# Attention products of a recurrent layer as 64x64 tiles in one TensorE visit per group, states added up outside of the matmuls, outputs split from PSUM, and a new list schedule

## The chip, the core and the metric

The kernel runs on one core of one Trainium2 chip. The metric is the device time of one launch in microseconds (us), the median of several runs; less is better. A core has a matrix engine (PE, with its own weight loads, PEld), a vector engine (DVE), an activation engine (ACT), a general engine (POOL) and a queue engine (SP) that issues DMA transfers. SBUF is the on-chip memory of 128 partitions, PSUM the eight banks into which PE writes.

## What is computed

A recurrent attention over 4 batches, 8 heads, 768 tokens and 48 channels a head, whose outputs feed a feed-forward layer with a 3-tap convolution over the tokens and a gate:

```
for t in range(S):
    kt, vt, rt = (k[:, :, t], v[:, :, t], r[:, :, t])
    cur = np.einsum('bhd,bhe->bhde', u[None] * kt, vt)
    y[:, :, t] = np.einsum('bhd,bhde->bhe', rt, state + cur)
    state = w[None, :, :, None] * state + np.einsum('bhd,bhe->bhde', kt, vt)
...
h = np.maximum(x @ w_in, 0.0)          # x: y with heads side by side, (4, 768, 384); w_in 384x1024
hp = np.concatenate([zeros, h, zeros], axis=1)
for k in range(K):
    conv_out += conv_w[k][None, None, :] * hp[:, k:k + S, :]
gate = 1.0 / (1.0 + np.exp(-conv_out))
return h * gate @ w_out                # w_out 1024x384
```

All tensors are fp32 (the weights of the feed-forward layer come as fp64 and are converted on the chip). For the feed-forward products each operand is split into a high and a low part of 32 bits, and three products (high x high, high x low, low x high) are added up.

## The kernel before

**The work.** There are 24 attention groups: each is 128 tokens of one batch with all 8 heads, as two chunks of 64 tokens. Heads lie in four pairs p; one head of a pair lies on partitions 64 and up, the other from 0. The feed-forward layer runs over *units* of tokens: batch 0 in three units of about 256, batches 1 to 3 in two units of 384. A unit has 8 steps f, one for each 128 of the 1024 columns. Such a step is called an iteration here; there are 72, the first 24 of them on the narrow units.

**An iteration.** `first(i)` (line 666) issues 9 matmuls into a PSUM bank HP (two banks, in turn; line 682), then on ACT the relu (L686) and the middle tap (L687), on DVE the two outer taps (L690, two instructions), on ACT the sigmoid (L693), on DVE the gate product (L694, the last reader of HP), on ACT the high part GH (L696), and on DVE or POOL the low part GL. `second(i)` issues 9 matmuls into the three output banks PO (L711), three iterations behind. After the eighth step of a unit ACT copies PO to OS and SP stores it.

**A group of attention.** `load(g)` brings k and r with channels on partitions (KR), with tokens on partitions (KT), and v (WW). `prep(g)` multiplies KR by powers of the decay (DVE), copies r into the stacked operands RA and RB (a DMA from SBUF to SBUF), scales KT into KTA and KTB (two more of these DMAs from group 8 on), and puts the diagonal term into RA and RB by a select on POOL (L560). `scores(g)` is 16 matmuls of 48 rows on four quarters of PE (L578 to L581), into the banks psC and psS. `masked(g)` copies the scores into RA and RB under a mask, in four DVE instructions (L590). `state(g, c)` is 8 matmuls into psS (L602, L603), of 112 and 128 rows, in which the decay of the old state stands as extra rows; ACT then copies the new state into the operands WW (L609, two instructions), for each of the two chunks. `outputs(g, c)` is 8 matmuls of 112 and 128 rows (L618, L619) into psY. `yout(g)` copies psY to YY on ACT (L628), and for every second group six small DMAs inside SBUF bring the rows of the fourth head pair to their places, then ACT (L639) and DVE or POOL split the result into the two parts of XT, the input of `first`.

The matmuls of attention are plain fp32: each appears in the trace as two records of PE.

**Two banks are shared.** psS takes the second half of the scores and the state; the masked copies of that half also take the lock of the state's copy:

```
lock = ["psAu" if o else "psBu"] if ps is psS else []
op("dve", 0.34, [key, "mask"], [("Rs", i, nm, q)] + lock, lambda e, T=T, r=r, o=o, ps=ps, n=n, q=q: V.copy_predicated(
```

**What sets the order.** The kernel's program is written down by a planner (class `Plan`): each operation is recorded with a duration for each engine that may run it, what it reads and writes, and a matmul column count. `late()` gives every operation a due time back from a row of PE work, less an offset for its kind (table `OFF`); `order()` takes the operations one at a time, on the engine that can begin first. What stands on an engine is then in fixed order, and waits there for its own inputs. All DMAs are issued from SP. Operations marked `any` go to DVE or POOL. Until the first product of `second`, the planner fills gaps of PE with products of zeros (L768).

The first matmuls of `first` need the weights of step 0 converted (`convert`, lines 471 to 492: ACT L481, DVE L483 and L485, ACT L491, DVE or POOL) and the XT of the first two groups. The conversions of the 16 weight pieces run beside the first unit.

## Time and profile before

| | us |
|---|---|
| three runs | 336.68, 338.31, 340.29 |
| median | 338.31 |
| span of the profiled execution | 336.5 |
| busy in it: PE, DVE, ACT, POOL | 305.0, 261.1, 215.3, 181.6 |
| first matmul of `first` starts at | 43.5 |
| last matmul of `second` ends at | 332.9 |

The profile is of one execution, and its own time is given as the span, from its first instruction to its last; that lies 1.8 us under the median and 0.2 us under the fastest of the three runs. The span's parts are read by stretches of time, engine by engine; PEclk is the share of full speed at which PE was clocked. L682 and the like are lines of the kernel before. A duration in the profile includes the engine's start-up and end, which overlap with those of its neighbours, so sums of durations come out some per cent over the busy time.

### The profile page before, as it was taken

The page shows a single profiled execution, that of the slowest core. Times are in us where ns is not written, and L with a number is a line of the kernel's source. Part 1 is how long each engine was busy: PE and PEld are TensorE (multiplying, and loading weights), DVE is VectorE, ACT ScalarE, POOL GpSimd, SP SyncE. Part 2 cuts the span into 40 slices and gives each one's busy share as a digit, 9 for nine tenths or more (in the row PEclk, how much of TensorE's full clock was granted, in tenths as well). Part 3 has the DMA queues.
Part 4 walks back from the last instruction along what each step waited for, and adds up shares of the span by engine and source line. Part 5 has one row for each costly group of instructions (what it writes and reads, how often), then busy time and mean ns, then how long its engine had stood idle before and what let it go on. Part 6 is the DMA issues. An engine that isn't in the chain of part 4 may idle for free.

```text
span 336.5 us, 9895 instructions
## 1 busy us (share of the span) xinstructions
PE 305.0 (91%) x3894; PEld 284.2 (84%) x3894; DVE 261.1 (78%) x459; ACT 215.3 (64%) x515; POOL 181.6 (54%) x211
## 2 busy tenths in 40 slices
PE   7879688779989899999899979999999999999995
PEld 3667677778888788899899979988899999999995
DVE  6969779889989999988899876867776755655550
ACT  3565476766766675576667836586776666865751
POOL 7869766768789787768561444233220123433230
PEclk9789699779999999999999999999999999999999
DMA  6989687643484859677555640362311100200101
GB/s 172 264 219 266 163 234 202 212 126 101 132 224 124 239 130 238 193 195 220 137 150 135 196 120 0 104 196 71 106 49 36 50 0 10 75 1 2 71 0 70
DMA packets 25118, 44.02 MB, mean 131 GB/s; under 512 B 5296, under 2 KB 16176, under 8 KB 25072
## 3 DMA queue, kind: packets, MB, share of 16 engines
q1 hardware_dynamic: 25072, 43.40, 46.0%
q8 instruction: 30, 0.49, 0.7%
q14 instruction: 16, 0.13, 0.1%
HBM read 30.01 MB, written 4.72 MB: 103 GB/s over the span
## 4 chain that ended last, share of the span: by engine, by line
PE 51%; DVE 17%; DMA 14%; ACT 9%; issue 5%; SPq 2%; POOL 2%; ACTq 0%; DVEq 0%; POOLq 0%
PE HP L682 21%; PE PO L711 19%; DMA KR<-in_krd_dram 7%; DVE KR L351 3%; DVE CV L690 3%; PE psS L602 3%; ACT WW L609 3%; DMA WW<-in_vt_dram 3%; PE psY L618 3%; DVE TT L485 2%; DMA ST<-in_w_in_dram 2%; SPq L354 2%; DVE RB L590 2%; ACT SG L693 1%; DVE RA L590 1%
## 5 line engine op out<-in xcount | busy, mean ns | idle before, releaser
L682 PE MATMUL HP<-XT,wi 128*128 128x386 f32 (+3 forms) x648 | 116.2, 326 | 8.6 <-DVE SG L694 8.5
L682 PEld LDWEIGHTS HP<-XT,wi 128*128 128x128 f32 x648 | 103.7, 190 | 11.9 <-DVE SG L694 11.0
L711 PE MATMUL PO<-GH,wo 128*128 128x384 f32 (+3 forms) x432 | 110.9, 323 | 0.0
L690 DVE SCALAR_TENSOR_TENSOR CV<-HP,cw,CV 128x384 f32<-128x384 f32 (+3 forms) x144 | 80.5, 568 | 23.6 <-ACT CV L687 22.1
L351 POOL TENSOR_TENSOR GL<-SG,GH 128x384 fp32r<-128x384 f32 (+3 forms) x51 | 47.7, 936 | 86.6 <-ACT GH L696 76.2
L711 PEld LDWEIGHTS PO<-GH,wo 128*128 128x128 f32 x432 | 77.3, 192 | 0.2
L711 PE MATMUL PO<-GL,wo 128*128 128x384 f32 (+3 forms) x216 | 69.8, 323 | 1.0 <-POOL GL L351 1.0
L693 ACT ACTIVATE SG<-CV 128x384 f32<-128x384 f32 (+3 forms) x72 | 35.1, 489 | 38.5 <-DVE CV L690 38.0
L694 DVE TENSOR_TENSOR SG<-HP,SG 128x384 f32<-128x384 f32 (+3 forms) x72 | 36.5, 509 | 18.4 <-ACT SG L693 17.3
L686 ACT ACTIVATE HP<-HP 128x386 f32<-128x386 f32 (+3 forms) x72 | 31.8, 442 | 24.7 <-PE HP L682 23.7
L711 PEld LDWEIGHTS PO<-GL,wo 128*128 128x128 f32 x216 | 41.4, 192 | 1.4 <-POOL GL L351 1.4
L696 ACT CAST GH<-SG 128x384 fp32r<-128x384 f32 (+3 forms) x72 | 34.0, 475 | 13.3 <-DVE SG L694 13.3
L687 ACT ACTIVATE CV<-HP,cw 128x384 f32<-128x384 f32 (+3 forms) x72 | 39.2, 545 | 1.7
L351 DVE TENSOR_TENSOR KR<-KR,TKR 112x1024 f32<-112x1024 f32 (+1 forms) x26 | 33.9, 1313 | 5.4 <-DMA KR<-in_krd_dram 5.0
L609 ACT COPY WW<-psS 48x192 f32<-48x192 f32 x88 | 27.5, 313 | 7.6 <-PE psS L603 6.1
L618 PE MATMUL psY<-RA,WW 112*48 112x64 f32 x384 | 27.3, 228 | 0.0
L560 POOL TENSOR_SCALAR_AFFINE_SELECT RA<-QQ 64x512 f32<-64x512 f32 x24 | 17.8, 743 | 17.6 <-PE psY L619 11.9
L619 PE MATMUL psY<-RB,WW 128*48 128x64 f32 x384 | 27.3, 228 | 0.0
L602 PE MATMUL psS<-WW,KTA 112*48 112x48 f32 x352 | 25.6, 218 | 0.5 <-ACT QQ L541 0.5
L603 PE MATMUL psS<-WW,KTB 128*48 128x48 f32 x352 | 25.6, 218 | 0.0
L618 PEld LDWEIGHTS psY<-RA,WW 112*48 112x48 f32 x384 | 24.5, 130 | 0.8 <-issue 0.5
L602 PEld LDWEIGHTS psS<-WW,KTA 112*48 112x48 f32 x352 | 20.1, 129 | 5.9 <-issue 2.5
(93 smaller groups left out, 549.5 us busy)
## 6 DMA issues: line engine op xcount, KB each, us to landing
KR<-in_krd_dram SPq DMA_DIRECT2D x24, 448.0 KB, 4.8
KT<-in_krt_dram SPq DMA_DIRECT2D x16, 384.0 KB, 5.0
WW<-in_vt_dram SPq DMA_DIRECT2D x48, 96.0 KB, 2.8
out_dram<-OS SPq DMA_DIRECT2D x18, 192.0 KB, 1.9
ST<-in_w_in_dram SPq DMA_DIRECT2D x8, 384.0 KB, 4.8
ST<-in_w_out_dram SPq DMA_DIRECT2D x8, 384.0 KB, 4.4
RA<-KR SPq DMA_DIRECT2D x22, 96.0 KB, 4.2
RB<-KR SPq DMA_DIRECT2D x22, 96.0 KB, 4.3
```

The source lines that it names most:

```text
L351: op(eng, d, rd, wr, lambda e: e.tensor_tensor(**kw), cls, port=True)
L602: PE.matmul(psS[64:112, n:n + D], KTA[i][:, p, c, :], WA[i][:, p, c, :], start=True, stop=True)
L609: lambda e, T=T, ps=ps, o=o: A.copy(T[j][o:o + 48, :, cn, :], ps[o:o + 48, 0:NP * D].rearrange("q (p d) -> q p d", p=NP)), "WS")
L618: PE.matmul(psY[64:112, n:n + C], WA[i][:, p, c, :], RA[i][0:112, p, t], start=True, stop=True)
L682: PE.matmul(hp, wi[a][:, j, fs], X[:, x, j, t], start=(j == 0 and k == 0), stop=(j == 2 and k == 2))
L686: op("act", act(n) - 0.042, [], [H_], lambda e: A.activation(hp, hp, AF.Relu, scale=1.0 / WS))
L687: op("act", act(n) + 0.05, [H_, "cw"], [("T", ti)], lambda e: A.activation(t1, hp[:, 1:n + 1], AF.Copy, scale=cw[:, 3 * f + 1:3 * f + 2]), ...
L690: op("dve", dve(n + 60), [H_, "cw"], [("T", ti)], lambda e, k=k: V.scalar_tensor_tensor(out=t1, in0=hp[:, k:n + k], scalar=cw[:, 3 * f + k ...
L693: op("act", act(n), [("T", ti)], [("SG", ti)], lambda e: A.activation(sg, t1, AF.Sigmoid))
L694: op("dve", dve(n), [H_], [("SG", ti)], lambda e: V.tensor_tensor(out=sg, in0=hp[:, 1:n + 1], in1=sg, op=ALU.mult), "GG")
L696: op("act", act(n), [("SG", ti)], [("GH", gi)], lambda e: A.copy(gh, sg))
L711: PE.matmul(PO[m][:, :n], wo[a][:, f, ms], g2[x], start=(f == 0 and k == 0), stop=(f == NF - 1 and k == 2))
```

## The change

Nearly all of the attention part is written anew; the iterations of the feed-forward layer keep their instructions (their shapes go from 384/384 to 382/386 columns on the wide units). The outputs, the scores and the *additions* k'v of a chunk are all made of operands that start at partition 0 or 64 and fill at most a 64x64 quarter of PE. The state is no longer in a matmul: DVE adds the additions from PSUM to the faded old state (SD, made on ACT, POOL or DVE).

```
-            op("pe", SCD, [("KK", i), ("RR", i)], ["psAs", "psBs", "psAu", "psBu", "psA4", "psB4"], mm, "sc", 768, visit=vis(g - 1, ORDER[3]))
-            for ps, n, nm, o, key, q in ((psC, 0, "a", 0, "psAs", 0), (psC, 0, "b", 64, "psBs", 0),
-                                         (psS, 4 * C, "a", 64, "psA4", 2), (psS, 4 * C, "b", 0, "psB4", 2)):
...
-                        PE.matmul(psS[64:112, n:n + D], KTA[i][:, p, c, :], WA[i][:, p, c, :], start=True, stop=True)
-                        PE.matmul(psS[0:48, n:n + D], KTB[i][:, p, c, :], WB[i][:, p, c, :], start=True, stop=True)
...
-                    op("act", 0.21, [], ["psAu" if nm == "a" else "psBu", ("WS", j, cn, nm)],
...
-            op("act", 0.48, ["psY"], [("YY", n, k), ("YY3", n)], lambda e: A.copy(
-                y[0:112, :, k, :], psY[0:112].rearrange("q (p t) -> q p t", p=NP)))
...
+        def scores(n):
+                        mms.append((ps[o:o + 64, m:m + C], KR[i][o:o + 48, 0, p, t], KR[i][o:o + 48, 1, p, t], True, True))
+        def additions(n):
+                        mms.append((ps[o:o + 48, m:m + D], KV[i][o:o + 64, 0, p, c, :], KV[i][o:o + 64, 2, p, c, :], True, True))
+        def outputs(g):
+                        mms.append((ps[64 - o:112 - o, m:m + C], KV[i][o:o + 64, 2, p, c, :], RS[j][o:o + 64, 2 * p + c, :], True, not inter))
+                            mms.append((ps[64 - o:112 - o, m:m + C], SS[j][o:o + 48, c, p, :], KR[i][o:o + 48, 1, p, t], False, True))
+        def visit(cls, *parts):
+                for k in range(0, max(len(direct), len(cross)), 2):
+                    for y, a, b_, s0, s1 in direct[k:k + 2] + cross[k:k + 2]:
+                        PE.matmul(y, a, b_, start=s0, stop=s1)
+        def faded(dst, src, rd, key):
+                    for p in range(NP):
+                        A.activation(dst[:, p], src[:, p], AF.Copy, scale=PW[:, p, 64:65])
+            op("any", {"dve": dve(192), "pool": pool(192), "act": 0.54}, rd + ["PW2"], [key], mul, "SD", port=True)
+        def chain(g):
+            op("dve", 0.73, [ka, "mask"], [("RS", j)], lambda e: V.copy_predicated(
+                faded(SD[0], SS[j][:, 0], [("S", j, 0)], ("SD", 0))
+                op("dve", dps(192), [ku, ("SD", 0)], [("S", j, 1)], lambda e: V.tensor_tensor(
+                    out=SS[j][:, 1], in0=ps[:, 0], in1=SD[0], op=ALU.add), "S1")
...
+        def split(g):
+            op("act", act(512), [key], [("X", b % 2, gi)], lambda e: A.copy(X[0:112, 0, :, t], y), "XH")
+            op("dve", dps(512), [key, ("X", b % 2, gi)], [("XL", b % 2, gi)], lambda e: V.tensor_tensor(
+                out=X[0:112, 1, :, t], in0=y, in1=X[0:112, 0, :, t], op=ALU.subtract), "XL")
+            for k in range(3):
+                for o in (0, 64):
+                    dma(ks, [("XM", b % 2, h, k, o)], F[o + 48:o + 64, :, k, tu], F[o + 16 * k:o + 16 * k + 16, :, 3, tu],
+                        32, (gi + 1 - cuts[h]) * 512, 0.6, "XM", g < EARLY)
...
+            visit("V", (0, scores(g + 1)), (0, additions(g + 1)), (1, outputs(g)))
```

Scores and additions are *direct* (rows and columns from the same o, 0 or 64), outputs are *cross* (rows from o, columns from 64 - o); the last group of a batch has no second chunk of additions. So a full visit issues 64 matmuls, two direct and two cross ones in turn: the scores (bank psA) and additions (psU) of the next group beside the outputs (psY) of this one. There are no operands RA, RB, KTA, KTB and YY and none of their DMAs. The diagonal term is made by a select on POOL, by one product on DVE, or by eight small activations on ACT (`DG`); fading takes four small activations where it falls to ACT. The diagonal sum is made by the matmul way (`q`, 16 matmuls of one column) only for groups 2 to 5 (before: groups 0 to 7); the other groups make it on POOL and DVE. The six DMAs that move the fourth pair's rows come once a unit, on both parts of XT. Weights may be loaded from ACT's DMA queue too. Units are cut at whole groups less two tokens. The planner's durations, offsets (now by three phases) and tie rules are other numbers, and three first groups use the still free banks HP and PO.

Counted from the two programs: the wide and narrow iterations are the same, 648 matmuls into HP and 648 into PO. Attention has 384 score, 352 state, 384 output and 128 one-column matmuls before; after it has 1472 in the visits and 64 one-column ones.

On PE, at the middle of a visit of the steady part, there stood before (psY the outputs, psC and psS the scores):

```order
L618 MATMUL psY<-RA_62,WW_77 48x64
L619 MATMUL psY<-RB_65,WW_77 48x64
L578 MATMUL psC<-KR_69 64x64
L579 MATMUL psC<-KR_69 64x64
L580 MATMUL psS<-KR_69 64x64
L581 MATMUL psS<-KR_69 64x64
```

and now stands (KV the tokens' k, r and v; RS the masked scores; SS the state; x2 is the pair on rows 0 and 64):

```order
L530 MATMUL psY<-RS_67,KV_66 48x64 x2
L530 MATMUL psA<-KR_61 64x64 x2
L530 MATMUL psY<-KR_63,SS_71 48x64 x2
L530 MATMUL psU<-KV_64 48x48 x2
L530 MATMUL psY<-RS_67,KV_66 48x64 x2
```

The outputs moved between the scores and additions of the next group, in fours; the state's matmuls are gone.

On DVE, over about one group of the steady part, there stood before (RA and RB take the masked copies, CV the taps, SG the gate products):

```order
L690 SCALAR_TENSOR_TENSOR CV_91<-HP_122,cw,CV_91 128x384
L590 COPY_PREDICATED RA_62<-mask,psC 64x256
L590 COPY_PREDICATED RA_62<-mask,psS 64x256
L590 COPY_PREDICATED RB_65<-mask,psS 64x256
L694 TENSOR_TENSOR SG_94<-HP_122,SG_94 128x384
L590 COPY_PREDICATED RB_65<-mask,psC 64x256
L351 TENSOR_TENSOR XT_90<-YY_88,XT_90 128x3x128
L351 TENSOR_TENSOR GL_106<-SG_94,GH_101 128x384
```

and now stands:

```order
L294 TENSOR_TENSOR KR_63<-KR_63,TKR 112x512 x2
L616 TENSOR_TENSOR SG_80<-HP_109,SG_80 128x382
L555 TENSOR_TENSOR SS_72<-psU,SD_73 112x192
L547 COPY_PREDICATED RS_68<-mask,psA 128x512
L569 TENSOR_TENSOR XT_75<-psY,XT_75 112x4x128
L294 TENSOR_TENSOR GL_90<-SG_80,GH_85 128x382
L612 SCALAR_TENSOR_TENSOR CV_78<-HP_108,cw,CV_78 128x382
L559 TENSOR_TENSOR SS_71<-psU,SD_74 112x192
```

Four masked copies became one; two state additions and a split that reads psY came in.

At the beginning of DVE's program, behind the reciprocal of the decay's powers, there stood before:

```order
L440 RECIPROCAL TKR<-PW 112x4x32
L446 TENSOR_TENSOR uw<-uc,wc 48x4 x2
L351 TENSOR_TENSOR KR_67<-KR_67,TKR 112x512 x2
L426 TENSOR_TENSOR PW<-PW 112x4x32
L426 TENSOR_TENSOR PW<-PW 112x4x31
```

and now stands:

```order
L392 RECIPROCAL TKR<-PW 112x4x32
L294 TENSOR_TENSOR KV_64<-KV_64,uu 128x384
L294 TENSOR_TENSOR KR_61<-KR_61,TKR 112x512
L462 TENSOR_REDUCE QQ_69<-KV_64 128x8
L294 TENSOR_TENSOR KR_61<-KR_61,TKR 112x512
```

The first scaling of KR moved behind a product that reads POOL's product of the loaded k and r.

More of the change, by code (lines that the diff above doesn't have):

```diff
@@ L105, in op @@
         self.port.append(port)
-        if visit is not None:
-            self.visits.setdefault(visit[0], []).append(n)
-            self.visit[n], self.rank[n] = visit
+        self.phases.append(self.phase)
+        if port == 2 and self.phase == 0:
+            self.pins[n] = len(self.pins) - 1e3
         return n
@@ L149, in order @@
         tick, cols, warm = 0, 0.0, False
-        seq, where, when = [], [None] * n, [None] * n
-        fill, hist = FILL, []
-        lanes = [0.0] * 7
-        mode, cur, slack = 0, None, SLACK
-        todo_v = {v: set(m) for v, m in self.visits.items()}
-        ext = {}
-        for v, m in self.visits.items():
-            inner = set(m)
-            for i in range(n):
-                if any(j in inner for j in ops[i][2]) and any(i in ops[k][2] for k in m):
-                    inner.add(i)
-            ext[v] = {j for k in m for j in ops[k][2]} - inner
-        end_of = [None] * n
-        todo = n
+        seq, where, when, end_of = [], [None] * n, [None] * n, [None] * n
+        fill, hist, lanes, dq = FILL, [], {v: [0.0] * (self.LANES - 1) for v in ("sp", "act")}, 0.0
+        dqa = 0.0
+        shared = 0.0
+        mode, todo = 0, n
         while todo:
@@ new lines, in rwkv_ffn_kernel @@
+        op("dve", 0.07, [], ["wc1"], lambda e: V.memset(wc, 1.0))
+        for o in (0, 64):
+            dma(["wc1"], [("wc", o)], wc[o:o + 48], wd[64 - o:112 - o], 48, 16)
+        for i in range(NBUF):
+            op("pool", 1.0, [], [("KZ", i)], lambda e, i=i: e.memset(KR[i][32:64], 0.0))
+        load(0)
+        load(1)
+        op("dve", 0.274, [], ["wz"], lambda e: V.memset(wz, 0.0))
+        op("act", 1.5, ["wz"], ["sgt"], lambda e: A.activation(cw[:, 0:1], wz[:, 0:1], AF.Sigmoid))
+        def warm(e):
+            for k in range(NW):
+                PE.matmul((psY, psU, HP[1], PO[0], PO[2])[min(k, 4)], wz[:, :128], wz, start=True, stop=True)
@@ L751, in rwkv_ffn_kernel, with follow, visits @@
-        for i in range(NI + LAG):
-            if i < NI:
+                    dma([("OS", q)], [("out", u, m)], out[ms, b * S + t0:b * S + t0 + n], o, 128, 4 * n, cls="out")
+        made = [0]
+        def follow(g):
+            group_phase(g)
+            if g + 1 < NG and g + 1 >= APART:
+                chain(g + 1)
+            split(g)
+            if g + NBUF < NG:
+                load(g + NBUF)
+            if g + 2 < NG:
+                prep(g + 2)
+        def visits(n):
+            while made[0] < min(n, NG):
+                g = made[0]
+                made[0] += 1
+                group_phase(g)
+                if g + 1 < APART:
+                    visit("VA", (0, scores(g + 1)))
+                    visit("VU", (0, additions(g + 1)))
+                    visit("VY", (1, outputs(g)))
+                    chain(g + 1)
+                elif g + 1 < NG:
+                    visit("V", (0, scores(g + 1)), (0, additions(g + 1)), (1, outputs(g)))
+                else:
+                    visit("V", (1, outputs(g)))
+                follow(g)
@@ new lines, in rwkv_ffn_kernel @@
+        plan.phase = 0
+        w_in_piece(0)
+        conv_piece()
+        w_out_piece(0)
+        for o in (0, 64):
+            dma([], [("uc", o)], uc[o:o + 48], ut[o].rearrange("p d -> d p"), 24, 4)
+            op("dve", 0.07, [("wc", o), ("uc", o)], [("uw", o)], lambda e, o=o: V.tensor_tensor(
+                out=uw[o:o + 48], in0=uc[o:o + 48], in1=wc[o:o + 48], op=ALU.mult))
+        load(2)
+        plan.phase = 0
+        prep(0)
+        plan.phase = 0
+        visit("VA", (0, scores(0)))
@@ L753, in rwkv_ffn_kernel @@
+        visit("VU", (0, additions(0)))
+        chain(0)
+        prep(1)
+        for k in range(1, WPRE):
+            w_in_piece(k)
+        for i in range(NU * NF + LAG):
+            x = (i + LEAD) / NF
+            u = int(x)
+            dn = NEED[min(u + 1, NU - 1)] - NEED[min(u, NU - 1)]
+            visits(NEED[min(u, NU - 1)] + sum(x % 1 >= (k + 0.5) / dn for k in range(dn)))
+            if i < NU * NF:
                 first(i)
+            plan.phase = min(2, 1 + i // 3)
             if i + WPRE < NF:
```

604 lines of the change are left out of this document (243 added, 361 removed), and 6 rows, old and new, of the table OFF.

## The prediction

> **What bounds the kernel now.** I read the stretches of time first, cut at the first gate product's end (51 us), the end of the narrow iterations (148), the 45th of the 72 gate products (231) and the last product into HP (323). Columns: stretch and length, then busy us and count for PE, PEld, DVE, ACT and POOL, then the granted clock, the DMA share and GB/s.
>
> ```profile
> core 0: us, PE busy (x) PEld busy (x) DVE busy (x) ACT busy (x) POOL busy (x), PEclk, DMA share, GB/s
> 0.00:51.00 51.00, 39.23 (x697) 31.15 (x698) 40.35 (x69) 28.40 (x74) 38.98 (x53) 0.87 0.82 220
> 51.00:148.00 97.00, 85.91 (x1372) 80.04 (x1373) 88.84 (x163) 64.16 (x172) 76.56 (x88) 0.96 0.62 172
> 148.00:231.00 83.00, 78.22 (x926) 73.70 (x927) 69.88 (x122) 54.71 (x124) 38.16 (x42) 1.00 0.50 141
> 231.00:323.00 92.00, 91.74 (x855) 89.72 (x850) 58.92 (x102) 63.60 (x138) 26.42 (x28) 1.00 0.14 42
> 323.00:336.50 13.50, 9.93 (x57) 9.60 (x55) 3.16 (x6) 4.40 (x9) 1.52 (x2) 0.99 0.12 44
> ```
>
> The overall shares (PE 305.0 of 336.5) would name PE as the bound; the stretches say something else. From 51 to 148 DVE is the fullest (88.84 of 97 us) and PE idles for 11. From 231 on PE is full (91.74 of 92). In between both are loaded. So the span is DVE's time up to the 45th gate product, and after it the PE work that is left. Here is the joint: the gate product frees its HP bank, and the next but one product of `first` begins behind it.
>
> ```profile
> 50.41 0.42 DVE L694 TENSOR_TENSOR SG<-HP,SG 128x254 f32<-128x254 f32 x1 [1.23 <-ACT SG L693]
> ...
> 230.34 0.56 DVE L694 TENSOR_TENSOR SG<-HP,SG 128x384 f32<-128x384 f32 x1 [0.59 <-ACT SG L693]
> ```
>
> DVE was busy for 40.35 + 88.84 + 69.88 = 199.1 us up to there and idle for 10.7 + 8.2 + 13.1 = 32. What it waited for, in the waits of the first, second and third stretch (total, times, longest):
>
> ```profile
> DVE RA L590 <- ACT WW L609: 1.9, 2, 1.3
> DVE KTA L351 <- PE psS L603: 1.0, 1, 1.0
> DVE RA L590 <- ACT WW L609: 3.3, 6, 1.0
> DVE KR L351 <- DMA KR<-in_krd_dram: 4.8, 4, 1.8
> ```
>
> The L609 rows are the shared bank psS: a masked copy waits until ACT has copied a state out of it.
>
> **The change, PE first.** A visit of before runs from its first state product to the first matmul behind it, 2.51 us where nothing stops it; and in the scores four quarters of PE already run side by side.
>
> ```profile
> 249.07 0.24 PE L602 MATMUL psS<-WW,KTA 112*48 112x48 f32 x1
> ...
> 251.58 0.45 PE L711 MATMUL PO<-GH,wo 128*128 128x384 f32 x1
> ```
>
> ```profile
> 210.25 0.22 PE L578 MATMUL psC<-KR 48*64 48x64 f32 x1
> 210.26 0.22 PE L579 MATMUL psC<-KR 48*64 48x64 f32 x1
> 210.27 0.22 PE L580 MATMUL psS<-KR 48*64 48x64 f32 x1
> 210.27 0.22 PE L581 MATMUL psS<-KR 48*64 48x64 f32 x1
> 210.31 0.22 PE L578 MATMUL psC<-KR 48*64 48x64 f32 x1
> ```
>
> Four records start in 0.02 us and the next four 0.06 us later (0.058 over several rounds). A full visit of after is 64 matmuls = 128 records = 32 rounds of four: 32 x 0.058 = 1.86, and with 0.25 for entering and leaving, 2.1 us. That is 0.4 less per visit, some 8 us over the 20 visits behind the first product of `first`.
>
> A rule speaks against these fours. The Trainium skill, page "TensorEngine Tiling (Array Packing)", section "Gotcha 1: PSUM Pressure", says that different row tiles cannot access the same PSUM bank at the same time; the direct pair and the cross pair each write one bank from two row tiles. By that rule a visit would take 3.7 + 0.25 us instead of 2.1. The trace disagrees: L578 and L579 are two row tiles that both write psC, 0.01 us apart.
>
> **DVE up to the 45th gate product.** The program order gives the counts up to it, before and after; the durations are the grouped rows by shape (xcount | busy us, mean ns):
>
> ```profile
> L351 DVE TENSOR_TENSOR KR<-KR,TKR 112x1024 f32<-112x1024 f32 x22 | 31.1, 1413 | 5.4 <-DMA KR<-in_krd_dram 5.0
> L690 DVE SCALAR_TENSOR_TENSOR CV<-HP,cw,CV 128x384 f32<-128x384 f32 x96 | 58.7, 615 | 22.5 <-ACT CV L687 21.2
> L694 DVE TENSOR_TENSOR SG<-HP,SG 128x384 f32<-128x384 f32 x48 | 26.7, 556 | 16.0 <-ACT SG L693 15.2
> L351 DVE TENSOR_TENSOR GL<-SG,GH 128x384 fp32r<-128x384 f32 x18 | 11.7, 650 | 2.1 <-ACT GH L696 1.6
> L590 DVE COPY_PREDICATED RB<-mask,psC 64x256 f32<-64x256 int32 x24 | 10.9, 454 | 0.6
> L545 DVE TENSOR_REDUCE QQ<-KT 128x8 f32<-128x384 f32 x16 | 8.7, 542 | 0.1
> L351 DVE TENSOR_TENSOR XT<-YY,XT 128x384 fp32r<-128x384 f32 x9 | 7.1, 788 | 1.0 <-ACT XT L639 0.9
> L351 DVE TENSOR_TENSOR KT<-KT,TH 128x384 f32<-128x384 f32 x5 | 3.8, 757 | 0.0
> L694 DVE TENSOR_TENSOR SG<-HP,SG 128x256 f32<-128x256 f32 x8 | 3.3, 417 | 0.4 <-ACT SG L693 0.2
> L351 DVE TENSOR_TENSOR KR<-KR,TKR 112x512 f32<-112x512 f32 x4 | 2.9, 762 | 0.0
> ```
>
> The two gate rows give the slope of an instruction that reads PSUM: (556 - 417) / 128 = 1.09 ns per column. In us:
> - masked copies: 80 of 256 columns become 22 of 512. The new one is not in the trace; its ends are 0.45 + 256 x 0.00109 = 0.73 and twice 0.45 = 0.90. I take 0.73, as a fixed part is paid once: -80 x 0.45 + 22 x 0.73 = **-19.9** (up to -16.2 at the other end);
> - KR: 21 x 1.413 + 4 x 0.762 = 32.7 becomes 46 x 0.73, between half of the long row (0.71) and the short row (0.76): **+0.9**;
> - state additions, 37 of 192 columns from PSUM: 0.417 - 64 x 0.00109 = 0.35 each: **+12.8**;
> - splits: 5 x 0.788 becomes 21 of 512 columns from psY, 0.556 + 128 x 0.00109 = 0.70: **+10.8** (POOL had done 13 of them);
> - 27 plain products (KT, KTA, KTB, KP, weights) become 12, at 0.757: **-11.4**;
> - 4 more reductions (0.542), 2 more taps (0.615), one more GL (0.650): **+4.1**.
>
> Sum: **-2.7**. Counted in full in this way, the records of before come to 213.5 up to here, 1.07 times the busy 199.1, so it is -2.5 busy: 196.6 us. The change moves PE's work, but hardly lightens DVE; its gain has to come from waits.
>
> **Waits.** First stretch: 10.7 idle, less the 1.9 and 1.0 for state copies and state products, makes 8. The new second place of the KR scaling behind a product of POOL may cost up to 2 there, and the other loads may come earlier by as much; I leave it at 8. Second and third stretch: without the 3.3 of L609, DVE was filled to 88.84 / 93.7 = 0.948 in the second. I take this for the third as well, where PE had been the other bound (78.22 of 83; now 0.4 a visit less): (196.6 - 40) / 0.948 = 165.2, so 8.6 idle. The other end is the fill of both stretches as they were, 158.7 / 180 = 0.88, which makes 21 idle. So the 45th gate product ends at 196.6 + 8 + 8.6 = **213**, before 231.
>
> **The PE work behind it.** These are the last pieces of the chain that ended last (start, length, what):
>
> ```profile
> 316.07 1.60 PE HP L682 x9
> 317.67 1.57 PE PO L711 x9
> ...
> 323.46 9.48 PE PO L711 x54
> ...
> 332.96 0.49 ACT OS L718
> ```
>
> By the order of after, 26 iterations of `first` are left (26 x 1.59 = 41.3), 98 triples of `second` (98 x 1.57 / 3 = 51.3), and three visits (the last has the outputs alone, still 32 rounds; 6.3): 98.9. From the last matmul (332.94) to the span's end are 3.6. For the kernel before the same count (26, 92, four visits and a half-group: 41.3 + 48.1 + 11) gives 104.0 with the 3.6, where the trace has 336.5 - 230.9 = 105.6; I add its 1.6. Sum: 213 + 98.9 + 3.6 + 1.6 = **317 us of span**, 19 under the 336.5 of the profiled execution. The median of the runs is 1.8 over that span, so I predict **319**, 6% less.
>
> **What is hidden.** ACT loses 88 state copies and the XT casts, and gains 104 + 104 activations of 64 and 48 columns, which the trace does not have; their nearest rows are below.
>
> ```profile
> L609 ACT COPY WW<-psS 48x192 f32<-48x192 f32 x88 | 27.5, 313 | 7.6 <-PE psS L603 6.1
> L541 ACT COPY QQ<-psC 128x8 f32<-128x8 f32 x8 | 1.3, 160 | 4.1 <-PE psC L539 4.0
> L489 ACT ACTIVATE cw<-TT 128x24 f32<-128x24 f32 x1 | 0.2, 223 | 0.4 <-DVE TT L485 0.4
> ```
>
> 208 x 0.16 to 0.22 is 33 to 46 us against at least 27.5 gone. I take 40; ACT had 33 us free in the second stretch and 28 in the third, so this is covered, unless the eight of a diagonal stand ahead of a sigmoid (1.3 to 1.8 us late for that iteration). POOL keeps its products and loses 30 of its 48 selects. SP loses 148 transfers inside SBUF (44 of r, 32 of k, 72 of the rows) and gets 50, with 4 on ACT's queue, so loads stand behind fewer issues; the 4.8 us of KR waits could go (a gain, not counted). The six row moves come once a unit, each landing in about 2.2 us:
>
> ```profile
> YY<-YY SPq DMA_DIRECT2D x72, 16.0 KB, 2.2
> ```
>
> The next unit's first product waits for all six. The order has a unit's groups done four or more iterations ahead, which covers 2.2 plus six issues; without that cover it is 5 us for each of 8 units.
>
> One more rule: the Trainium skill, "SBUF — State Buffer", section "Who interferes with whom", says that a DVE instruction with at most one SBUF input does not contend with GpSimd. By it the new splits and additions stay at 0.70 and 0.35; by the old split's row (two SBUF inputs, 0.548 to 1.176) 21 of them would cost 2 more.
>
> **Rivals.** (1) *PE-bound throughout*, chance 0.16. If DVE's durations fall to their least (KR's short ones are 0.678 against the 0.73 taken) and loads are never late, PE's own sum decides. Before, the first product began at 43.5:
>
> ```profile
> L682 PE MATMUL HP<-XT,wi x648: 275/337/583, 43.5 to 323.1; 128*128 128x386 f32 x108, 128*128 128x256 f32 x18, 128*128 128x258 f32 x18, 128*128 128x260 f32 x18
> ```
>
> In after's DVE order only some 35 instructions, about 18 us of work, stand ahead of the second split; with 8 idle and 4 for the moves it can start at 30. Then 48 x 3.16 + 24 x 2.11 = 202, 21 visits = 44, two q = 2, the tail and lost clock 6.6, 5 of stalls: about 290 to 296. Against it: DVE must give up 20 us.
> (2) *The fours do not overlap*, 0.08: the change does not do what it says. A visit costs 1.86 more, 21 x 1.86 = 39 on PE, and PE's path is 30 + 248 + 39 + 12 = 329, so 328 to 333.
> (3) *More waits on fixed orders*, 0.10: DVE's fill stays at 0.88: 317 + 12 and the 1.8, 329 to 333.
> (4) *Slower: the clock*, 0.06. PE gets fuller gaps between 30 and 130 us, and from the first product into PO on nothing fills them. Its work there is 24 x 2.11 + 9 x 2.1 + 3 = 73 us at full clock. At half clock throughout it is 146, the narrow iterations end at 176 instead of some 130 (148 less 6 of waits and 12 of DVE work that the order puts later), and the time is about 365; below a mean clock of about 0.6 in this stretch it is slower than before. For it: 0.87 in the first stretch. Against: 0.96 in the second, with 11 us of gaps.
>
> **Chances.** Forecast 0.60 (306 to 328). A measurement here can tell about 1%, 335 to 342 being no change. Faster by over 1%: 0.87, the forecast, (1), and most of (2) and (3); same 0.06; slower 0.07. The range reaches into (1) and (3): **300 to 333**, about one in ten left out on each side.
>
> **What would show it.** Right: the 45th gate product near 213, DVE over 0.93 full from 45 to 210, visits of 2.1 us, no wait of a masked copy on ACT, PE full from there on. Wrong: visits near 4 us; PEclk under 0.8 between 40 and 130; DVE waiting for SD or RS; or PE full already from 150 on, which would make it faster than I say.

## The result, and the profile after

The changed kernel takes **317.2 us** (median of five runs, 316.5 to 318.9; the kernel before 337.7 in five): a ratio of 0.939 (95% interval 0.934 to 0.945), 6% faster. The forecast was 319, with a range of 300 to 333. In a later session the same kernel took 317.6 (ratio 0.947, 0.942 to 0.953). The span of the profiled execution is 316.9 us, where the sum had 317; this execution was the slowest of the five, and the other four had spans of 314.6 to 315.6, so for a usual execution the sum is some 2 us too high. The landmarks in between were off by 4 us in both directions.

These are the stretches of the changed kernel, cut at its own first gate product, at the end of the narrow iterations, at the 45th gate product and at the last product into HP. The columns are those of the same view in the prediction.

```profile
0.00:48.20 48.20, 38.48 (x663) 30.16 (x664) 33.89 (x66) 24.35 (x77) 26.18 (x41) 0.86 0.79 201
48.20:131.80 83.60, 75.34 (x1556) 70.34 (x1555) 79.24 (x153) 64.09 (x194) 61.94 (x61) 1.00 0.53 145
131.80:217.00 85.20, 81.20 (x1495) 76.61 (x1497) 83.08 (x144) 67.86 (x193) 48.90 (x50) 1.00 0.51 139
217.00:300.00 83.00, 83.00 (x714) 82.26 (x703) 55.76 (x97) 55.98 (x124) 13.75 (x14) 1.00 0.09 26
300.00:316.90 16.90, 13.46 (x76) 13.14 (x75) 4.47 (x7) 5.56 (x12) 1.02 (x1) 0.97 0.19 69
```

DVE is busy for 33.89 + 79.24 + 83.08 = 196.2 us up to the 45th gate product, before 199.1: it did not get lighter. Its idle time there went from 32 to 21 us, of which only 6.5 lie behind the first gate product (before 21). In the third stretch DVE is full to 98% (83.08 of 85.20; before 69.88 of 83), and PE too is full to 95%. From 217 to its last matmul PE never stops. Of the 19.6 us that the span lost, 13.8 were gained up to the 45th gate product (217.1; before 230.9) and 5.8 behind it.

What ends the waits of DVE, then of PE, from the first to the 45th gate product (total, times, longest):

```profile
DVE KR L294 <- DMA KR<-in_krd_dram: 1.6, 2, 0.8
DVE CV L612 <- ACT CV L609: 1.4, 5, 0.4
DVE SG L616 <- ACT SG L615: 0.9, 1, 0.9
DVE RS L547 <- ACT RS L474: 0.7, 1, 0.7
...
PE HP L601 <- DVE SG L616: 7.1, 10, 1.6
PE PO L634 <- ACT OS L641: 3.3, 2, 1.8
```

No masked copy waits for a state copy any more (the one of 0.7 waited for a diagonal), and PE's largest wait is for DVE's gate product. A visit now looks so, its first foursome and the first rows behind its first round (start, length):

```profile
164.48 0.27 PE L530 MATMUL psA<-KR 48*64 48x64 f32 x2
164.49 0.26 PE L530 MATMUL psY<-RS,KV 64*48 64x64 f32 x2
164.59 0.22 PE L530 MATMUL psA<-KR 48*64 48x64 f32 x1
```

This visit began at 164.48 and the product of `first` behind it at 166.44: 1.96 us.

The groups of DVE by shape (count, busy us, mean ns):

```profile
L294 DVE TENSOR_TENSOR KR<-KR,TKR 112x512 f32<-112x512 f32 x48 | 44.8, 938 | 3.5 <-DMA KR<-in_krd_dram 3.5
L547 DVE COPY_PREDICATED RS<-mask,psA 128x512 f32<-128x512 int32 x22 | 16.1, 730 | 0.7 <-ACT RS L474 0.7
L569 DVE TENSOR_TENSOR XT<-psY,XT 112x512 fp32r<-112x512 f32 x23 | 15.7, 681 | 0.3 <-ACT XT L568 0.2
L294 DVE TENSOR_TENSOR GL<-SG,GH 128x382 fp32r<-128x382 f32 x13 | 10.7, 830 | 1.9 <-ACT GH L618 1.6
L559 DVE TENSOR_TENSOR SS<-psU,SD 112x192 f32<-112x192 f32 x19 | 6.6, 347 | 0.3 <-ACT SD L538 0.3
```

The operations that were not in the trace of before cost what was taken for them (0.730 for 0.73, 0.681 for 0.70, 0.347 for 0.35); KR, which was in it, costs 0.938 for 0.73.

One place the prediction had not costed. In the first stretch ACT issues four of the six row moves of the first unit from its own DMA queue:

```profile
24.89 5.52 ACTq L298 DMA_DIRECT2D XT<-XT  x4
30.46 0.17 ACT L458 COPY QQ<-PO 128x8 f32<-128x8 f32 x1 [8.29 <-DMA XT<-XT]
```
```profile
30.67 1.97 PE L530 MATMUL PO<-KR 48*64 48x64 f32 x32 [4.40 <-ACT QQ L458]
...
42.09 2.67 PE L601 MATMUL HP<-XT,wi 128*128 128x256 f32 x18
```

The four issues take 5.5 us together (0.59 to 0.72 each, with pauses between them), ACT does nothing else meanwhile, and PE waits for the small copy of QQ behind them. The first product begins at 42.1, hardly earlier than before (43.5).

### The profile page after: what moved, and what is told of

Its sections match the earlier page's. It is cut to its first block, busy times and chain, and to the rows that moved or that the text cites. A ratio compares the mean times of both kernels' runs of the same rounds, so it can differ in the third digit from the quotient of the medians.

```text
span 316.9 us, 10888 instructions
## 1 busy us (share of the span) xinstructions
PE 291.5 (92%) x4483; PEld 272.5 (86%) x4483; DVE 256.4 (81%) x464; ACT 217.8 (69%) x596; POOL 151.8 (48%) x166
## 4 chain that ended last, share of the span: by engine, by line
PE 50%; DVE 24%; DMA 9%; ACT 6%; POOL 4%; issue 4%; SPq 2%; ACTq 0%; DVEq 0%; POOLq 0%
PE PO L634 20%; PE HP L601 19%; PE psY L530 5%; DMA KV<-in_krt_dram 5%; DVE CV L612 5%; DVE KR L294 4%; DMA KR<-in_krd_dram 3%; DVE TT L419 3%; DVE GL L294 3%; POOL KV L294 2%; ACT RS L474 2%; DVE SG L616 2%; DVE TT L417 2%; PE psA L530 2%; SPq L298 2%
## 5 line engine op out<-in xcount | busy, mean ns | idle before, releaser
L601 PE MATMUL HP<-XT,wi 128*128 128x384 f32 (+4 forms) x648 | 114.9, 325 | 7.1 <-DVE SG L616 7.1
L634 PE MATMUL PO<-GH,wo 128*128 128x382 f32 (+4 forms) x432 | 111.1, 322 | 4.0 <-ACT OS L641 3.3
L612 DVE SCALAR_TENSOR_TENSOR CV<-HP,cw,CV 128x382 f32<-128x382 f32 (+4 forms) x144 | 80.7, 567 | 13.7 <-ACT CV L609 12.6
L294 POOL TENSOR_TENSOR GL<-SG,GH 128x382 fp32r<-128x382 f32 (+4 forms) x41 | 39.5, 963 | 95.5 <-ACT GH L618 87.1
L634 PE MATMUL PO<-GL,wo 128*128 128x382 f32 (+4 forms) x216 | 69.3, 321 | 0.4 <-POOL GL L294 0.4
L615 ACT ACTIVATE SG<-CV 128x382 f32<-128x382 f32 (+4 forms) x72 | 35.0, 487 | 27.8 <-DVE CV L612 26.8
L616 DVE TENSOR_TENSOR SG<-HP,SG 128x382 f32<-128x382 f32 (+4 forms) x72 | 36.5, 507 | 15.8 <-ACT SG L615 15.6
L294 DVE TENSOR_TENSOR KR<-KR,TKR 112x512 f32<-112x512 f32 x48 | 44.8, 938 | 3.5 <-DMA KR<-in_krd_dram 3.5
L530 PE MATMUL psY<-RS,KV 64*48 64x64 f32 x736 | 43.8, 222 | 0.0
L530 PE MATMUL psY<-KR,SS 48*48 48x64 f32 x672 | 41.1, 219 | 0.0
L608 ACT ACTIVATE HP<-HP 128x384 f32<-128x384 f32 (+4 forms) x72 | 31.6, 440 | 13.8 <-PE HP L601 12.8
L609 ACT ACTIVATE CV<-HP,cw 128x382 f32<-128x382 f32 (+4 forms) x72 | 39.1, 544 | 1.3
```

Source lines behind the costliest of these rows:

```text
L294: op(eng, d, rd, wr, lambda e: e.tensor_tensor(**kw), cls, port=True)
L530: PE.matmul(y, a, b_, start=s0, stop=s1)
L601: PE.matmul(hp, wi[a][:, j, fs], X[:, x, j, t], start=(j == 0 and k == 0), stop=(j == 2 and k == 2))
L608: op("act", 0.093 + n / 1200.0, [], [H_], lambda e: A.activation(hp, hp, AF.Relu, scale=1.0 / WS))
L609: op("act", 0.158 + n / 1200.0, [H_, "cw"], [("T", ti)], lambda e: A.activation(t1, hp[:, 1:n + 1], AF.Copy, scale=cw[:, 3 * f + 1:3 * f + ...
L612: op("dve", 0.117 + n * 1.085e-3, [H_, "cw"], [("T", ti)], lambda e, k=k: V.scalar_tensor_tensor(out=t1, in0=hp[:, k:n + k], scalar=cw[:, ...
```

## The experiments

The theory under test is the prediction's, that DVE bounds the kernel up to the 45th gate product; that PE follows closely behind was added after the first runs. The rivals are that PE is the bound there already, or that the fours on PE play no part. In all variants of the changed kernel the order of the program on each engine is that of the changed kernel, except for what the diff shows. The words "the stretch" below mean the time from the end of the first to the end of the 45th gate product, in the profiled execution: 169.3 us in the changed kernel, with DVE busy for 162.9.

### Pairs in place of fours

```
-                for k in range(0, max(len(direct), len(cross)), 2):
-                    for y, a, b_, s0, s1 in direct[k:k + 2] + cross[k:k + 2]:
-                        PE.matmul(y, a, b_, start=s0, stop=s1)
+                for y, a, b_, s0, s1 in direct + cross:
+                    PE.matmul(y, a, b_, start=s0, stop=s1)
```

> The changed kernel with the visits' matmuls issued in another order alone: all direct ones, then all cross ones, so that two quarters of PE run side by side in place of four. In the trace of the changed kernel a visit in fours takes 1.96 us and 32 records in pairs took 0.92, so a visit should take 3.7 to 3.9: +1.8 for each of 18 visits up to the 45th gate product (+33) and +4 behind it. Theory (DVE sets the end up to that product, at 217 us, and PE has 12 us of idle time between the first gate product and it): PE becomes the bound, those 12 us are eaten and the rest shows, 338 to 346 us, slower than or equal to the kernel before the change. Rival (the shorter visits had no part in the gain, it is all waits of DVE): under 325. Rival 2 of the prediction gave 328 to 333.

Measured: 338.3 us, ratio to the kernel before 1.001 (0.997 to 1.006). The whole gain is gone, as the theory had it (338 to 346). The second and third stretch of this variant, in an execution of 340.9 us:

```profile
50.00:141.00 91.00, 87.13 (x1519) 84.09 (x1521) 78.11 (x154) 63.72 (x193) 60.74 (x61) 0.96 0.49 136
141.00:238.00 97.00, 95.86 (x1576) 92.18 (x1572) 81.71 (x147) 70.19 (x196) 49.61 (x51) 1.00 0.46 124
```

PE is now the full engine (95.86 of 97) and DVE idles for 15 us there. A visit runs from 178.69 to 182.17, 3.5 us:

```profile
178.69 0.39 PE L529 MATMUL psA<-KR 48*64 48x64 f32 x6
...
182.17 0.44 PE L600 MATMUL HP<-XT,wi 128*128 128x388 f32 x1
```

So a foursome saves 1.5 us a visit, not the 1.8 expected, and the rival that the fours had no part falls. The Trainium skill's rule that the prediction weighed ("TensorEngine Tiling (Array Packing)", "Gotcha 1: PSUM Pressure", that two row tiles cannot access one PSUM bank at the same time) gave 3.95 us for a visit in fours; it takes 1.96, and only the visit in pairs comes near that figure, so the trace does not agree with the rule here. The two tiles of a pair write different partitions of the bank; what two tiles on the same partitions would do, no run here shows.

### The masked copy in four pieces, as before

```
-            op("dve", 0.73, ..., lambda e: V.copy_predicated(out=RS[j], mask=mask..., data=pa...), "RS")
+            op("dve", 0.73, ..., lambda e: [V.copy_predicated(
+                out=RS[j][o:o + 64, n:n + NP], mask=mask[o:o + 64].unsqueeze(1).broadcast_to([64, NP, C]),
+                data=pm[o:o + 64, n:n + NP]) for n in (0, NP) for o in (0, 64)], "RS")
```

> The changed kernel with its one masked copy of 128x512 undone into four of 64x256, in the same place and over the same data. In the trace the new copy takes 0.62 us from its start to the next one's, the four of the kernel before 0.47 each: +1.25 for each of the 20 copies up to the 45th gate product, +25 of DVE work. Theory (DVE is the bound up to there, idle for 7 us of the 169 between the first and the 45th gate product): the 45th gate product goes from 217 to 235 to 242, and the time to 335 to 342. Rival (PE, idle for only 4 of the 85 us between 132 and 217, is the bound there, DVE only full beside it): less than half of it shows, 322 to 329.

Measured: 331.0 us, ratio 0.981 (0.975 to 0.986), 13.8 more than the changed kernel; the stretch took 180.7, 11.3 longer, with DVE busy for 176.0.

```profile
139.00:230.00 91.00, 84.34 (x1579) 78.00 (x1578) 89.59 (x176) 68.90 (x194) 49.15 (x49) 1.00 0.50 136
```
```profile
L548 DVE COPY_PREDICATED RS<-mask,psA 64x256 f32<-64x256 int32 x88 | 39.2, 445 | 1.0
L294 DVE TENSOR_TENSOR GL<-SG,GH 128x382 fp32r<-128x382 f32 x13 | 8.7, 668 | 1.5 <-ACT GH L619 1.5
```

DVE is full to 98%, and most of what is added to its busy time (13.1) shows in the stretch (11.3): DVE is the bound, not PE. The result lies between the two expectations because the price was wrong: the copies did add 18.9 us of DVE's time, but KR and GL gave 7 of them back (GL 0.668 for 0.830): of the 17 GL in the stretch, 6 are longer than 0.72 us, where the changed kernel has 14. That such long ones come from POOL's products is shown further below.

### Less work on DVE, less on PE, and both

```
-            ..., "KR", out=v, in0=v, in1=W.unsqueeze(2).broadcast_to([112, NP, 2, C]), op=ALU.mult)
+            ..., "KR", out=v[:, :, 0], in0=v[:, :, 0], in1=W, op=ALU.mult)                 # kr_half
...
-                for k in range(0, max(len(direct), len(cross)), 2):
+                for k in range(0, n // 2 if half else n, 2):        # visit_half: half = from the eighth visit on
```

> The changed kernel with the scaling of KR on the first of each group's two chunks alone, 256 of 512 columns (the second chunk stays unscaled); nothing else changes. In the trace an undisturbed one takes 0.60 us from start to start and the mean record 0.93: -0.30 to -0.45 for each of 46, 14 to 20 us of DVE work less up to the 45th gate product. Theory (DVE is the bound up to there): the product comes earlier until PE stops it. PE waits for DVE's gate products for 7.1 us of the second stretch and idles for 4 of the third; so 7 to 12 us less, 305 to 310, with PE full from the second stretch on. Rival (PE is the bound from 132 us on): only the second stretch can gain, and with the stalls on row moves and OS left, 313 to 316.

> The changed kernel, where the visits from the eighth on issue only the first half of their matmuls (the second chunk's products are left out): 16 rounds of fours in place of 32, -0.93 us for each of 17 visits, of which about 14 (13 us) lie between the seventh group and the 45th gate product at 217, and the rest behind it. Theory (DVE is the bound up to there): those 13 us turn into idle time of PE, and only the 2 to 3 us behind 217 show, with up to 2 more: 312 to 315. Rival (PE is the bound from 132 on): 10 to 15 us less, 302 to 307.

> The two halvings at once: KR scaled on one of two chunks (alone: 312.6 us, the 45th gate product 165.2 us behind the first one in place of 169.3, DVE idle for 13.1 in place of 6.5), and the visits from the eighth on with the first half of their matmuls (alone: 315.8, 168.6 us, no change). Second theory, after these two runs: up to the 45th gate product DVE is the bound, but PE follows so closely that 4 us less of DVE's time hand the bound to PE. Then both together free the 16 us of KR: the stretch from the first to the 45th gate product takes 153 to 158 us, and the time is 299 to 306 us. Rival (something else stops DVE 4 us earlier, late loads of KR and the chain of an iteration through ACT): no more than kr_half and visit_half added, 163 to 165 us and 310 to 312.

Measured: kr_half 312.6 us (0.927, 0.922 to 0.932), visit_half 315.8 (0.934, 0.928 to 0.941), both_half 307.8 (0.921, 0.913 to 0.928). The third stretch of the three, about:

```profile
129.00:212.00 83.00, 81.19 (x1560) 77.10 (x1563) 76.69 (x145) 68.58 (x195) 47.63 (x48) 1.00 0.54 144
```
```profile
126.00:212.00 86.00, 76.93 (x973) 71.44 (x977) 83.47 (x145) 67.81 (x193) 50.47 (x50) 0.96 0.53 139
```
```profile
123.00:204.00 81.00, 76.41 (x1001) 70.87 (x999) 76.99 (x147) 67.42 (x190) 52.02 (x53) 1.00 0.55 148
```

Half of the matmuls of most visits taken away lowers the visits' PE time in the stretch by 10.6 us (26.8 for 37.4) and leaves the stretch at 168.6 (169.3). PE idles for 5 us more there; the rest stands beside a lower granted clock (0.97 in the stretch, 1.00 in the changed kernel). DVE stays full, so PE's work is not the bound up to the 45th gate product. Lightening DVE by 10.8 us, however, shortens the stretch by only 4.1, below the 7 to 12 expected; then PE is full in the third stretch (81.19 of 83), and the 312.6 us lie nearer to the rival's 313 to 316 than to the theory's 305 to 310. Both together shorten the stretch by 10.3, which is twice the sum of the two alone (4.9) but short of the 11 to 16 expected, and the 307.8 us lie between the two expectations. So PE follows DVE within about 4 us: a gain on DVE hands the bound to PE.

### The kernel before, lightened on either engine

```
-            "KR", out=kr, in0=kr, in1=TKR...unsqueeze(2).broadcast_to([112, 2 * NP, 2, C]), ...
+            "KR", out=kr[:, :, 0], in0=kr[:, :, 0], in1=TKR..., ...                         # before_dve_light
...
-                for p in range(NP):
+                for p in range(1 if g > 7 else NP):            # before_pe_light, in outputs and state
```

> The kernel before the change, with the scaling of KR of the long form (112x1024) on the first of each group's two chunks alone, 512 columns (the other stays unscaled): an undisturbed one goes from 1.14 us to about 0.6, and 17 of them lie between the first and the 45th gate product: 9 to 12 us of DVE work less. Prediction's step (DVE is the bound up to there): 6 to 10 less, 328 to 332. Rival (PE is the bound from 148 on): only the part before 148 shows, 2 to 5 less, 333 to 336.

> The kernel before the change, with the outputs and the state products of only one of the four head pairs from the ninth group on (the rest is left out): in its trace these matmuls take 17.2 us of PE from 51 to 148 us and 11.6 from 148 to 231, so about 8.7 us less in the latter stretch, 4 in the former and 3 behind. It asks what bounded the kernel before between its gate products. Prediction's step (DVE sets the end up to the 45th gate product): the 3 behind it show, and up to 3 more, 332 to 336. Rival (PE, idle for 4.8 us from 148 to 231 where DVE idles for 13.4, was the bound of that stretch): 10 to 15 less, 322 to 328.

Measured: before_dve_light 334.0 us (0.992, 0.986 to 0.998), before_pe_light 334.7 (0.993, 0.987 to 1.000). With DVE lighter by 10.7 us in the stretch, this became 4.6 us shorter (175.5 for 180.1), and the rest turned into idle time, in the third stretch beside a PE that was full:

```profile
143.00:224.00 81.00, 79.07 (x911) 74.47 (x910) 66.20 (x123) 55.23 (x126) 39.00 (x45) 1.00 0.52 149
```

The 334.0 us lie in the rival's range, not in the prediction's (328 to 332). So in the kernel before, DVE was the bound only in part; some of what is missing may be the clock, which was 0.96 in this stretch against 0.98. How large PE's part was stays open. The 334.7 us are in the range of the prediction's step (332 to 336), but the variant with the lighter PE lost its clock: its ten runs went from 329.9 us at a mean granted clock of 0.972 to 342.0 at 0.918. Its PEclk row (granted clock in tenths, 40 slices of the span), and under it that of the kernel before:

```profile
PEclk9797587979997999599699799979879999999999
```
```profile
PEclk9789699779999999999999999999999999999999
```

### The row moves on SP

```
-                    plan.ops[i][3](eng[where[i]])
+                    plan.ops[i][3](SP if plan.ops[i][4] == "XM" else eng[where[i]])
```

> The changed kernel with the four row moves of the first unit that stand on ACT's DMA queue issued from SP, at the same place of the program; no other instruction moves. In the trace of the changed kernel ACT issues nothing else from 24.89 to 30.41 us, its copy of QQ waits 8.3 us for that, PE 4.4 for the copy and DVE 3.2 for a conversion. Theory: this waiting is on the path of the first stretch, so the first product begins 3 to 5 us earlier (42.1 to 38 us), and since DVE is full from there to the 45th gate product all of it is kept: 312 to 314.5 us, against 317.2. Rival (the moves and the loads behind them on SP are late in place of ACT, six issues of 0.7 to 1.2 us): 316 to 319.

Measured: 313.0 us, ratio 0.934 (0.926 to 0.941), in the theory's range. The six issues, the copy of QQ and the first product of `first`:

```profile
24.56 5.23 SPq L298 DMA_DIRECT2D XT<-XT  x6
```
```profile
24.91 0.17 ACT L458 COPY QQ<-PO 128x8 f32<-128x8 f32 x1 [3.50 <-PE PO L456]
```
```profile
35.98 2.62 PE L601 MATMUL HP<-XT,wi 128*128 128x256 f32 x18
```

The copy comes 5.5 us earlier and the first product 6.1. The stretch is the same (169.1), so all of it is kept. Executions differ in the first stretch: with the moves on ACT the first gate product ended between 43.4 and 49.8 us in nine profiles (mean 46.6), with the moves on SP at 41.6 and 42.7. The 4 to 5 us are therefore the better size. This version is faster than the kernel before, and its times lie under the changed kernel's; its interval overlaps the changed kernel's first one (0.934 to 0.945) a little, and the next experiment looks at it again on one chip.

The runs leave a rival for the cause of these 4 to 5 us. PE's granted clock was 0.50 from 29.1 to 42.8 us in the changed kernel, and here only from 31.4 to 34.8. The PEclk rows of the changed kernel and of this one:

```profile
PEclk9998589999999999999999999999999999999999
PEclk9999799999999999999999999999999999999999
```

The eleven profiles of the changed kernel and its variants go with this time at half clock. The first product began at 41.8 to 44.3 us where it lasted 13.7 us, at 40.2 and 40.5 with 10.2, at 37.2 to 40.0 with 6.8, and at 36.0 with 3.4. Among those with 6.8, the one with the moves on SP (gl_pool, 37.2) is hardly ahead of visit_half (37.3) with the moves on ACT, although its copy of QQ came 4.3 us earlier. So the earlier copy is shown, and the earlier first product only together with a shorter time at half clock. Whether PE's shorter wait for the copy is what kept the clock up was not tested.

### GL on POOL as well

```
+   ... G if plan.ops[i][4] == "GL" ...
```

> moves_sp (row moves of the first unit on SP, alone 313.0 us) and with it every low part GL of the gate product on POOL, at its place in the program: 17 of them stood on DVE up to the 45th gate product, where they took 15.1 us of its busy time, 0.89 each. Theory (DVE is the bound up to there, PE some 4 us behind it): the stretch from the first to the 45th gate product goes from 169.1 to 163 to 166 us, PE being the next bound, and the time to 307 to 311. Rival (what POOL takes over comes back as longer records of DVE, since the other products of DVE with two operands in SBUF grow beside POOL's, and products of second wait for a late GL): 312 to 318.

> The changed kernel itself once more, beside the two below on one chip, since executions of a kernel differ by 2 to 3 us in the first stretch (first gate product at 43 to 50 us in six profiles of kernels with the same beginning). No theory speaks on it: 315 to 319 us, ratio 0.935 to 0.945. It is the measure for the next one.

Measured: gl_pool 313.5 us (0.932, 0.928 to 0.937), and the changed kernel beside it on the same chip 317.6 (0.947, 0.942 to 0.953), in the range of times expected, its ratio a little over. So the gain of moves_sp shows again (4.1 us), and GL on POOL adds nothing to it. Against moves_sp, DVE became 8.3 us lighter in the stretch, which went only from 169.1 to 167.4 us: it idles for 13.8 us in place of 7.2, with waits for ACT that were not there before (the largest one in the third stretch is quoted), and KR got longer, to a mean of 1.01 us:

```profile
DVE XT L569 <- ACT XT L568: 3.0, 3, 2.1
```
```profile
L294 DVE TENSOR_TENSOR KR<-KR,TKR 112x512 f32<-112x512 f32 x48 | 48.3, 1011 | 2.2 <-DMA KR<-in_krd_dram 2.1
```

The time is the rival's; of the 15 us taken off DVE, KR gave back 5 (30.4 to 35.5 us of records in the stretch), and most of the rest became idle time.

### Without a product of POOL

```
             tt("any", 384, ["TH"], [("Kt", i)], "KT", ...)
+            if g > 5:
+                plan.ops[-1] = plan.ops[-1][:3] + (lambda e: None,) + plan.ops[-1][4:]
```

> The changed kernel without POOL's product of KV with TH (128x384, 1.07 us) from the seventh group on, which is left out; no DVE instruction changes. In the trace of the changed kernel 28 of the 48 KR records take 0.67 to 0.69 us and the others up to 2.95, the long ones beside products of POOL; counted over the undisturbed length, DVE's records are 23.7 us longer between the first and the 45th gate product, 5.3 of them beside this product. Theory (POOL's products hold DVE up, and DVE is the bound): the mean KR record falls to 0.80 to 0.88, the stretch between the two gate products from 169.3 to 164 to 167 us, and the time to 312 to 315. Rival (the long records only show DVE waiting for something it would have waited for anyway): no change of the stretch beyond 1 us, 316 to 318.

Measured: 311.5 us, ratio 0.928 (0.921 to 0.935), and the stretch at 164.9. No DVE instruction was changed, and yet DVE was busy for 7.1 us less:

```profile
L294 DVE TENSOR_TENSOR KR<-KR,TKR 112x512 f32<-112x512 f32 x48 | 42.5, 891 | 4.7 <-DMA KR<-in_krd_dram 4.7
L294 DVE TENSOR_TENSOR GL<-SG,GH 128x382 fp32r<-128x382 f32 x13 | 8.5, 656 | 2.0 <-ACT GH L620 1.6
```

KR fell less than expected (0.891, not 0.80 to 0.88), GL more (0.656 for 0.830): of the records that DVE lost in the stretch, GL gave 5.4 us and KR only 1.4. The stretch is as the theory had it, and the time a little under its 312 to 315. POOL's products do hold DVE up. How, two places of the changed kernel show; first DVE, then POOL:

```profile
202.23 2.95 DVE L294 TENSOR_TENSOR KR<-KR,TKR 112x512 f32<-112x512 f32 x1
```
```profile
201.22 1.47 POOL L540 TENSOR_TENSOR SD<-SS,PW 112x192 f32<-112x192 f32 x1
202.65 1.00 POOL L294 TENSOR_TENSOR GL<-SG,GH 128x382 fp32r<-128x382 f32 x1
203.62 1.02 POOL L294 TENSOR_TENSOR KV<-KV,TH 128x384 f32<-128x384 f32 x1
```

```profile
104.61 1.33 DVE L294 TENSOR_TENSOR KR<-KR,TKR 112x512 f32<-112x512 f32 x1
```
```profile
104.40 1.00 POOL L294 TENSOR_TENSOR KV<-KV,uu 128x384 f32<-128x384 f32 x1
105.36 1.46 POOL L294 TENSOR_TENSOR KV<-KV,TH 128x384 f32<-128x384 f32 x1
```

In the first place the KR product starts while POOL is at work, POOL's three stand back to back to 204.64, and KR ends at 205.18, 0.54 later: it waited for all three. In the second it ends at 105.94, 0.54 behind the first of POOL's two, and here the second is the longer one. All 18 KR records of over 0.72 us end 0.53 to 0.55 us behind the end of a POOL product. Of the nine that met POOL's products back to back, three waited for all of them and six for the first alone; what decides this stays open. The Trainium skill, "SBUF — State Buffer", "Who interferes with whom", calls the port pair that the two share an exclusive lock, and says that a DVE instruction with at most one input in SBUF does not contend. The trace agrees with both: KR's end 0.54 us behind POOL's is what a wait for the lock would give, and the splits and state additions, which read PSUM, kept to 0.68 and 0.35.

### Pairs and four masked copies together

> The changed kernel with both undone at once: the visits in pairs (alone 338.3 us, 21 over the changed kernel; the stretch from the first to the 45th gate product 186.9 us with DVE idle for 28) and the masked copy in four (alone 331.0, 14 over it; 180.7 us, DVE idle for 5). Theory (two bounds close to each other; in pairs PE is the bound): the 13 us of DVE work find room in the 28 idle ones, so the time is 338 to 343 us and the one masked copy is worth at most 4 us without the fours. Rival (the two are gains of one chain through both engines and add up): 350 to 354.

Measured: 343.2 us, ratio to the kernel before 1.022 (1.016 to 1.027). Beside pairs alone that is 4.8 more by the times, 2% or nearly 7 us by the ratios of the two sessions, and 4.7 in the stretch (191.6 for 186.9), where beside fours the same edit cost 13.8. Both engines are heavily loaded in its third stretch:

```profile
141.00:238.00 97.00, 95.02 (x1532) 90.94 (x1530) 91.02 (x174) 70.24 (x195) 48.09 (x48) 1.00 0.46 124
```

Nearer to the theory (338 to 343, at most 4) than to the sum (350 to 354), though a little outside it. The one masked copy is worth 14 us with the fours and 5 to 7 without them.

## Why the prediction was right, point by point

**The bound in the changed kernel: right.** DVE up to the 45th gate product, PE behind it: shown by visit_half (nothing gained in the stretch), mask4 (paid for the most part) and a PE without a gap after 217. **The bound in the kernel before: too simple.** before_dve_light got 4.6 us out of 10.7. The sentence that DVE hardly gets lighter, so that the gain has to come from waits, is right as a sum, but pairs shows what it hides: with visits of 3.5 us DVE idles for 28 us in the stretch. So the waits could go because PE's visits became shorter.

**The visits: right**, 2.0 us for 2.1. **The terms of DVE: the new ones right, KR and GL too small.** The masked copy, the splits, the additions and the reductions (0.541) came to within 0.02 us. KR up to the 45th gate product took 42.8 us of records in place of 46 x 0.73 = 33.6, GL 16.2 in place of 12.5: the step that failed is "between half of the long row and the short row", which priced an instruction by its length alone, though its time depends on what POOL does beside it. By records the sum was 10.6 short (221.4 in place of 210.8), and came out right in busy time (196.2 for 196.6) only because the records overlapped more, 1.13 times the busy time and not 1.07. That was luck: the prediction gave no reason for another overlap.

**The waits of DVE.** Second and third stretch: 6.5 us for 8.6, right. First stretch: 14 for 8, and a first product at 42 where rival (1) had 30. The step that failed is the line on hidden things, where the four issues on ACT's queue were noted as a relief of SP; what they do to ACT was not counted, and PE waited 4.4 us behind them. How much of the 6 us comes from this alone stays open: moves_sp got rid of them, but with less time at half clock. Less the 2 us saved behind the first gate product, they make the 4 us by which the 45th gate product came late (217.1 for 213). In the second session's profile it came at 214.9.

**The PE work behind it.** 99.8 us in place of 104.0, so this error cancelled the one just named, by luck. The counts of matmuls of `first`, `second` and the visits behind 217.1:

```profile
217.10:316.90 99.80, 45.60 (x234) 41.55 (x234) 0.99 0.11 33
```
```profile
217.10:316.90 99.80, 53.36 (x279) 49.38 (x279) 0.99 0.11 33
```
```profile
217.10:316.90 99.80, 5.36 (x268) 4.91 (x258) 0.99 0.11 33
```

The 26 iterations of `first` are there, but 279 / 3 = 93 triples, not 98, and the visits take 5.4 us, not 6.3; of the 1.6 us of stalls that were added, about 1 is left. The step that failed is the count of triples. In the order on PE 98 of them stand behind the start of iteration 46 and 93 behind that of iteration 47, which is the first one that needs the 45th gate product; the five between them were done before 217.1. They are 2.6 of the 4 us.

**What was to be hidden.** ACT's small activations take 0.25 us from start to start (eight in 2.02 us), so 52 us and not 40; they are covered all the same, with ACT idle for 19 and 17 us in the two stretches. The row moves of the later units take 3.8 to 6.1 us of SP for six issues, and no product waits for them.

**The rivals.** PE-bound throughout and fours that do not overlap: both refuted by runs. More waits on fixed orders: refuted by the 98% of DVE. The clock: 1.00 from the first gate product to 300 us, so it did not come. In the second session it was 0.93 in the narrow iterations and 0.98 from there to the 45th gate product, and the stretch still took only 170.1 us.

## What to carry to other kernels

Where two engines are nearly equally full, price an edit by what the other engine allows, and try the opposite edit too: 10.8 us off DVE shortened the stretch by 4, 10.6 off PE's visits by less than 1, both by 10. Look at the DMA issues on a compute engine's queue as at its instructions, and at who waits behind them: ACT ran nothing else during its four. A product of two operands in SBUF had no fixed price beside POOL's products (KR took 0.67 to 2.95 us), so price it from rows with the same neighbours. And where executions of one kernel differ, compare the granted clock before a difference is put down to the edit.

## What the runs showed of the hardware

A DVE product with both inputs in SBUF that met POOL's products ended a fixed time behind the end of one of them: KR took 0.68 us alone, and all 18 longer ones ended 0.53 to 0.55 us behind a POOL product. Up to three POOL products back to back were waited for (2.95 us), but in six cases of nine only the first. Leaving out one kind of POOL product freed 7 us of DVE.

PE was clocked at half speed for 3.4 to 13.7 us of the first stretch behind 26 us, and the first product came later the longer this lasted (36.0 to 44.3 us). In before_pe_light, with less work on PE, the mean granted clock of the ten executions was 0.944, against 0.967 in the 23 of the kernel before. That half visits lower it in the changed kernel is not shown: visit_half had 0.98 and 0.96 in its second and third stretch, but the unchanged kernel had 0.94 and 0.98 in the second session.

A row move of 32 rows took 0.59 to 0.73 us to issue in most records, a weight piece of 128 rows mostly 0.33 to 0.49; with the pauses between them four moves held ACT for 5.5 us, and six held SP for 5.2.
